# Loading k and v with the token halves of half of the heads exchanged, so that scores skip the masked quarter from tile 6 on, and splitting u and w1 with fewer ScalarE products

## The chip, the cores and the metric

The kernel runs on one core of one Trainium2 chip. The metric is the device time of one execution in microseconds (us), taken from several executions. A *fast* run is one in the undisturbed state; all medians, lowest and highest values below are of fast runs.

## The reference, cut to what matters

Two blocks follow each other. The first is a linear attention with decay (4 batches, 8 heads, 768 tokens, 64 values per head), whose output is laid out as x with 512 columns. The second is a mixing step on x, ending in two large products with w_ch1 (512x2048) and w_ch2 (2048x512).

```python
for b in range(nb):                                   # blocks of tokens
    qb, kb, vb = (q[:, :, sl], k[:, :, sl], v[:, :, sl])
    intra = einsum('bhic,bhjc->bhij', qb, kb) * Dmask     # scores, causal mask with decay
    intra = einsum('bhij,bhjd->bhid', intra, vb)
    inter = einsum('bhid,bhde->bhie', qb * lam_pow, kv_state)
    out[:, :, sl] = intra + inter
    kv_state = lam_block * kv_state + einsum('bhsd,bhse->bhde', kb * rev_pow, vb)
...
u = x + (x.T @ U @ V).T
return u + maximum(u @ w_ch1, 0) @ w_ch2
```

The kernel works in tiles of 128 tokens: 6 per batch, 24 in all. In a tile's 128x128 scores of one head the quarter "late keys, early queries" is wholly masked. That quarter is what the change leaves out.

## The kernel before

Per tile there are three loads (q, k, v), each of all 8 heads: 128 partitions (tokens) by 8 heads by 64 values, 256 KB. Only the loads of the very first tile's q and k are cut in two.

```python
def load(name, s, engine):
    b, c = divmod(s, NT)                                   # NT = 6 tiles per batch
    t = raw_pool.tile([P, H, D], FP32, tag=f"{name}raw", bufs=4 if name == "k" else 3, ...)
    source = {"q": q, "k": k, "v": v}[name]
    n = H if name == "v" else H // parts(s)
    for h in range(0, H, n):
        engine.dma_start(out=t[:, h : h + n, :],
            in_=source[b, h : h + n, c * P : (c + 1) * P, :].rearrange("h p d -> p h d"))
    raw[s, name] = t
...
def load_next(name, engine=nc.sync):                       # all but the very first k on the SyncE queue
    if waiting[name]:
        load(name, waiting[name].pop(0), engine)
```

`load_next` is called where a buffer comes free: q's and k's after the tile's transposes, v's after the state product. The kernel's program order on SyncE is therefore also the order of its DMA queue. The weights' loads ("words") and the stores of finished u tiles stand in the same queue:

```python
def turn(s):
    ...                                                    # 4 transposes on TensorE
    nc.sync.dma_start(out=u_d[s], in_=xs.pop(s))           # frees one of the 9 buffers of x
    ...
def intra(s):
    ...                                                    # 32 passes into px
    xs[s] = x_pool.tile([P, C], FP32, tag="x", name="x_nat")   # bufs=9
    nc.scalar.copy(xs[s].rearrange(...), px)               # ScalarE empties px
```

The scores, and the splitting of u into a high and a low part for the large products:

```python
def scores(s):
    ...
    for a in range(HP):                                    # 4 pairs of heads
        for x in range(2):
            for rows in half if s >= 2 * NT else [slice(0, P)]:
                nc.tensor.matmul(out=pss[rows, x, a, :], lhsT=kt[half[x], a, rows],
                                 rhs=qt[half[x], a, :], start=True, stop=True)
...
    te = tmp("te").rearrange(...)
    nc.scalar.mul(te, t, E)                                # E = 1/4096
    nc.scalar.copy(hi, t)
    nc.gpsimd.tensor_tensor(out=diff, in0=te, in1=low.bitcast(FP32), op=ALU.subtract)
```

## Time and profile before

| | before |
|---|---|
| median of 3 runs | 676.5 us (676.48 to 676.61) |
| span of the profiled run | 674.7 us |
| attention (start to the first instruction of the large products) | 123.3 us |
| DMAs that SyncE issues in attention | 99 |
| time that these issues took | 75.6 us of 123.3 |

The prediction below shows the page, the stretches and the chain. Two views more are needed here. The first is SyncE's own timeline (start, length, line, operation, tile): early in the kernel, where issues stand in a row, and at 82 us, where they come after pauses.

```profile
5.04 0.85 SPq L267 DMA_DIRECT2D kraw<-in_k_dram  x1
5.94 0.85 SPq L267 DMA_DIRECT2D vraw<-in_v_dram  x1
6.83 0.85 SPq L139 DMA_DIRECT2D words<-in_moe_U_dram  x1
...
82.70 0.37 SPq L267 DMA_DIRECT2D qraw<-in_q_dram  x1
83.18 0.52 SPq L267 DMA_DIRECT2D kraw<-in_k_dram  x1
84.93 0.37 SPq L267 DMA_DIRECT2D vraw<-in_v_dram  x1
```

In the early row an issue takes 0.85 us; at 82 us q's and v's take 0.37 after a pause, and k's 0.52, 0.11 us behind q's. The pauses are visible as SyncE's own waits (what its queue waited for: total us, times, longest):

```profile
SPq L267 <- PE pkv L406: 19.7, 14, 3.7
...
SPq L267 <- PE pq L343: 10.4, 10, 2.0
```

In this trace SyncE waits some 30 us for buffers to come free, so it seems to have time to spare. Whether issue times can be read like this is taken up again under whole_loads, where the same 99 DMAs took longer to issue.

### The profile page before, as it was taken

To read this page: it belongs to the slowest core of one execution; us is meant where nothing else is said; L and a number is where in the kernel's file an instruction comes from. 1 tells how busy PE (TensorE), PEld (TensorE's weight loads), DVE (VectorE), ACT (ScalarE), POOL (GpSimd) and SP (SyncE) were. 2 spreads that over 40 slices of the span, in tenths; PEclk is the share of its full clock that TensorE was granted. 3 is DMA by queue.
4 is the path that set the end of the run, shared out by engine and by line. 5 is a ranking of instruction groups with operands and counts; after the bars stand their busy time and mean duration, and the time that the engine had idled before them with its cause. 6 is when DMAs were issued, how large, how long until landed. Compare 5 with 4: busy or idle time off the path is not lost.

```text
span 674.7 us, 13222 instructions
## 1 busy us (share of the span) xinstructions
PE 666.1 (99%) x5124; PEld 545.0 (81%) x5124; DVE 500.1 (74%) x879; ACT 293.3 (43%) x545; POOL 113.8 (17%) x92
## 2 busy tenths in 40 slices
PE   9999999999999999999999999999999999999997
PEld 8888888887888888888888888888888888888885
DVE  5689999777999777777797255786586775865864
ACT  4666878555665544444455121232232322322320
POOL 4556667330000000000000000030030200300300
PEclk9999999999999999999999999999999999999999
DMA  9999894164777655555577999854253363453421
GB/s 203 223 235 248 207 221 124 64 223 155 243 256 244 221 202 204 203 204 203 202 266 258 324 329 373 294 168 154 94 203 109 110 203 94 159 153 95 163 86 63
DMA packets 131776, 131.28 MB, mean 195 GB/s; under 512 B 81346, under 2 KB 89794, under 8 KB 131714
## 3 DMA queue, kind: packets, MB, share of 16 engines
q1 hardware_dynamic: 130656, 130.18, 60.5%
q8 instruction: 40, 0.66, 0.4%
q10 hardware_dynamic: 1058, 0.26, 0.2%
q14 instruction: 22, 0.18, 0.1%
HBM read 80.09 MB, written 50.33 MB: 193 GB/s over the span
## 4 chain that ended last, share of the span: by engine, by line
PE 93%; DVE 3%; ACT 2%; issue 0%; DMA 0%; SPq 0%; DVEq 0%; ACTq 0%
PE pz L709 27%; PE pz L841 13%; PE pz L843 13%; PE pd L719 13%; PE pd L845 13%; PE pss L388 3%; PE px L441 3%; PE put L511 1%; PE pq L343 1%; PE pkv L406 1%; PE px L429 1%; PE pk L343 1%; DVE sm L397 1%; PE pp L456 1%; PE pu L494 1%
## 5 line engine op out<-in xcount | busy, mean ns | idle before, releaser
L709 PE MATMUL pz<-u_hl,w 128*128 128x512 f32 x768 | 190.5, 397 | 0.0
L709 PEld LDWEIGHTS pz<-u_hl,w 128*128 128x128 f32 x768 | 144.0, 188 | 35.5 <-issue 0.4
L841 PE MATMUL pz<-w_hl,m 128*128 128x512 f32 x384 | 151.6, 396 | 0.0
L843 PE MATMUL pz<-w_hl,m 128*128 128x512 f32 x384 | 151.6, 396 | 0.0
L845 PE MATMUL pd<-w_d,m 128*128 128x512 f32 x384 | 150.0, 396 | 0.0
L824 ACT ACTIVATE m<-mt 128x512 fp32r<-128x512 f32 x96 | 60.7, 632 | 195.4 <-PE pd L845 144.6
L825 DVE SCALAR_TENSOR_TENSOR m<-rm,m 128x512 fp32r<-128x512 f32 x96 | 71.5, 746 | 50.1 <-ACT m L824 49.9
L870 POOL TENSOR_TENSOR o<-o,u 128x512 f32<-128x512 f32 x20 | 29.8, 1522 | 447.4 <-DVE o L866 447.4
L724 DVE SCALAR_TENSOR_TENSOR r<-pd,r 128x512 f32<-128x512 f32 x96 | 61.8, 686 | 54.7 <-ACT r L715 43.6
L719 PE MATMUL pd<-u_d,w 128*128 128x512 f32 x384 | 98.6, 397 | 0.0
L843 PEld LDWEIGHTS pz<-w_hl,m 128*128 128x128 f32 x384 | 72.3, 188 | 17.7
L845 PEld LDWEIGHTS pd<-w_d,m 128*128 128x128 f32 x384 | 72.3, 188 | 17.6
L841 PEld LDWEIGHTS pz<-w_hl,m 128*128 128x128 f32 x384 | 72.3, 188 | 17.6
L719 PEld LDWEIGHTS pd<-u_d,w 128*128 128x128 f32 x384 | 72.1, 188 | 17.3
L715 ACT ACTIVATE r<-pz 128x512 f32<-128x512 f32 x96 | 52.0, 594 | 60.0 <-PE pz L709 60.0
L826 DVE SCALAR_TENSOR_TENSOR m<-m 128x512 fp32r<-128x512 f32 x96 | 69.2, 721 | 0.9
L823 DVE TENSOR_SCALAR mt<-rm 128x512 uint32<-128x512 uint32 x96 | 46.2, 481 | 28.2 <-DMA rm<-r_d 27.7
L204 ACT CAST w<-wt 128x512 fp32r<-128x512 f32 x32 | 19.9, 622 | 40.9 <-DVE wt L201 33.7
L397 DVE TENSOR_TENSOR sm<-pss,mask 128x512 f32<-128x512 f32 x48 | 30.8, 684 | 5.3 <-PE pss L388 5.2
L371 POOL TENSOR_TENSOR qs<-qt,powq 128x512 f32<-128x512 f32 x20 | 26.0, 1298 | 23.9 <-ACT qt L346 20.0
L441 PEld LDWEIGHTS px<-vraw,sm 128*64 128x64 f32 x768 | 24.7, 137 | 6.3 <-issue 2.4
L159 ACT ACTIVATE sc<-sc,ends 128x512 f32<-128x512 uint32 x30 | 21.7, 723 | 18.2 <-DVE sc L153 18.2
(84 smaller groups left out, 710.2 us busy)
## 6 DMA issues: line engine op xcount, KB each, us to landing
r_d<-r SPq DMA_DIRECT2D x96, 256.0 KB, 2.3
rm<-r_d SPq DMA_DIRECT2D x96, 256.0 KB, 2.7
words<-in_moe_w_ch_dram SPq DMA_DIRECT2D x30, 512.0 KB, 4.4
w_d<-w SPq DMA_DIRECT2D x16, 768.0 KB, 3.3
w_hl<-w_d SPq DMA_DIRECT2D x16, 512.0 KB, 6.4
vraw<-in_v_dram SPq DMA_DIRECT2D x24, 256.0 KB, 4.1
u_d<-x_nat SPq DMA_DIRECT2D x24, 256.0 KB, 3.2
u<-u_d SPq DMA_DIRECT2D x24, 256.0 KB, 4.0
```

Source lines behind the costliest of these rows:

```text
L441: nc.tensor.matmul(out=px[half[t], x, a, :], lhsT=sm[:, x, a, half[t]], rhs=vr[:, 2 * a + x, :], start=(first and a == 0), stop=(a == HP - 1),
L709: nc.tensor.matmul(out=acc[g][0], lhsT=w[:, n, ct, :], rhs=uhl[g][:, n, ct, :], start=(ct == 0 and n == 0), stop=(ct == CT - 1 and n == 1),)
L715: nc.scalar.mul(rs[g], acc[g][0], 1.0 + E)
L719: nc.tensor.matmul(out=acc[g][1], lhsT=w[:, 2, ct, :], rhs=ud[g][:, ct, :], start=(ct == 0), stop=(ct == CT - 1),)
L724: nc.vector.scalar_tensor_tensor(rs[g], acc[g][1], 4096.0, rs[g], ALU.mult, ALU.add)
L823: nc.vector.tensor_scalar(t.bitcast(U32), r.bitcast(U32), HI, None, ALU.bitwise_and)
L824: nc.scalar.activation(out=m[:, 0], in_=t, func=AF.Relu)
L825: nc.vector.scalar_tensor_tensor(m[:, 1], r, 0.0, hi, ALU.max, ALU.subtract)
L826: nc.vector.scalar_tensor_tensor(m[:, 2], hi, E, low, ALU.mult, ALU.subtract)
L841: nc.tensor.matmul(out=pz, lhsT=m[:, 0, cols], rhs=hl[:, 0], start=first, stop=False)
L843: nc.tensor.matmul(out=pz, lhsT=m[:, 1, cols], rhs=hl[:, 1], start=False, stop=end)
L845: nc.tensor.matmul(out=pd, lhsT=m[:, 2, cols], rhs=dd, start=first, stop=end)
```

## The change

Its intent has two parts.

*Scores.* From tile 6 on the masked quarter is skipped by giving each head two passes: early keys against 128 queries, late keys against 64. To balance the quarters of the array, two of the four pairs of heads keep their tokens with the halves exchanged. This is done in the load: k and v of heads 4 to 7 come in two DMAs of 64 partitions, each landing in the other half. Each k or v load thus becomes three DMAs: 128 partitions of heads 0 to 3, and 64 + 64 partitions of heads 4 to 7. The bytes stay the same. The mask of these heads is built from a turned identity.

*Splitting.* u's high part is kept divided by 4096, which saves ScalarE the product `te`; w1's low part is written by VectorE itself, which saves another ScalarE product.

```diff
@@ load
-        source = {"q": q, "k": k, "v": v}[name]
-        n = H if name == "v" else H // parts(s)
+        source = {"q": q, "k": k, "v": v}[name][:, :, c * P : (c + 1) * P, :]
+        n = H // parts(s) if name == "q" else H // 2
         for h in range(0, H, n):
-            engine.dma_start(
-                out=t[:, h : h + n, :],
-                in_=source[b, h : h + n, c * P : (c + 1) * P, :].rearrange("h p d -> p h d"),
-            )
+            rows = [(slice(0, P), slice(0, P))]
+            if name != "q" and h > 0:
+                rows = [(half[0], half[1]), (half[1], half[0])]
+            for to, of in rows:
+                engine.dma_start(
+                    out=t[to, h : h + n, :],
+                    in_=source[b, h : h + n, of, :].rearrange("h p d -> p h d"),
+                )
@@ scores
-        for a in range(HP):
+        for a in (0, 2, 1, 3):
+            first, last = half[::-1] if a in turned_a else half
+            both = [(first, slice(0, P)), (last, half[1])]
             for x in range(2):
-                for rows in half if s >= 2 * NT else [slice(0, P)]:
+                for rows, cols in both if s >= NT else [(slice(0, P), slice(0, P))]:
                     nc.tensor.matmul(
-                        out=pss[rows, x, a, :], lhsT=kt[half[x], a, rows],
-                        rhs=qt[half[x], a, :], start=True, stop=True,
+                        out=pss[rows, x, a, cols], lhsT=kt[half[x], a, rows],
+                        rhs=qt[half[x], a, cols], start=True, stop=True,
@@ splitting of u
-            te = tmp("te").rearrange("p (c n) -> p c n", n=P)
-            nc.scalar.mul(te, t, E)
-            nc.scalar.copy(hi, t)
-            nc.gpsimd.tensor_tensor(out=diff, in0=te, in1=low.bitcast(FP32), op=ALU.subtract)
+            nc.scalar.mul(hi, t, E)
+            nc.gpsimd.tensor_tensor(
+                out=diff, in0=hi.bitcast(FP32), in1=low.bitcast(FP32), op=ALU.subtract
+            )
@@ the first product's evacuation
-            nc.scalar.mul(rs[g], acc[g][0], 1.0 + E)
+            nc.scalar.mul(rs[g], acc[g][0], 4096.0 + 1.0)
```

Cut: the parameter by which w1 gets the new splitting and w2 keeps its old one, the turned identity and its scans, and keeping one score buffer for all tiles (so that the skipped quarter holds finite numbers).

More of the change, by code (lines that the diff above doesn't have):

```diff
@@ L187, in weight_steps, with split_steps @@
         return fetches + [one, two, three, four]
-    def split_steps(tile_of, src, in_parts=False):
+    def split_steps(tile_of, src, in_parts=False, scale=None):
         st = {}
@@ L206, in six @@
         def six():
-            w = st["w"]
-            nc.vector.tensor_tensor(out=w, in0=w, in1=st["t"], op=ALU.subtract)
-            on_scalar(lambda: nc.scalar.mul(st["o"][:, 1, :], w, 4096.0))
+            w, low = st["w"], st["o"][:, 1, :]
+            st["low"] = low.bitcast(FP32) if scale is None else w
+            nc.vector.tensor_tensor(
+                out=low if scale is None else w, in0=w, in1=st["t"], op=ALU.subtract
+            )
+            if scale is not None:
+                on_scalar(lambda: nc.scalar.mul(low, w, scale))
         def seven():
             nc.vector.scalar_tensor_tensor(
-                st["o"][:, 2, :], st["t"], -E, st["w"], ALU.mult, ALU.add
+                st["o"][:, 2, :], st["t"], -E, st["low"], ALU.mult, ALU.add
             )
@@ L250, in bank @@
         return psa[0].tile(shape, FP32, tag=tag, bufs=2, name=name)
+    half = [slice(0, D), slice(D, P)]
+    turned_a = range(HP // 2, HP)
     lamb = consts.tile([P, H], FP32, name="lamb")
@@ L285 @@
     mask = consts.tile([P, 2, HP, P], FP32, name="mask")
+    ident_turned = consts.tile([P, P], FP32, name="ident_turned")
     rev = small[:, 8:16].rearrange("p (x a) -> p x a", x=2)
@@ L297, in constants @@
                 nc.vector.tensor_tensor_scan(
-                    mask[:, x, a, :], lamb[:, h : h + 1].broadcast_to([P, P]), ident, 0.0,
-                    ALU.mult, ALU.add,
+                    mask[:, x, a, :], lamb[:, h : h + 1].broadcast_to([P, P]),
+                    ident_turned if a in turned_a else ident, 0.0, ALU.mult, ALU.add,
                 )
@@ L323 @@
     st = {}
+    scores_of = []
     kv = {}
-    half = [slice(0, D), slice(D, P)]
     def keep_busy(n):
@@ L383, in scores @@
         qt, kt = st[s]["qt"], st[s]["kt"]
-        st[s]["pss"] = pss = two_banks("pss", "pss").rearrange("p x (a i) -> p x a i", a=HP)
-        for a in range(HP):
+        if s == 0:
+            scores_of.append(two_banks("pss", "pss").rearrange("p x (a i) -> p x a i", a=HP))
+        pss = scores_of[0]
+        for a in (0, 2, 1, 3):
+            first, last = half[::-1] if a in turned_a else half
+            both = [(first, slice(0, P)), (last, half[1])]
             for x in range(2):
-                for rows in half if s >= 2 * NT else [slice(0, P)]:
+                for rows, cols in both if s >= NT else [(slice(0, P), slice(0, P))]:
                     nc.tensor.matmul(
-                        out=pss[rows, x, a, :], lhsT=kt[half[x], a, rows],
-                        rhs=qt[half[x], a, :], start=True, stop=True,
+                        out=pss[rows, x, a, cols], lhsT=kt[half[x], a, rows],
+                        rhs=qt[half[x], a, cols], start=True, stop=True,
                     )
     def masked(s):
-        pss = st[s].pop("pss")
+        pss = scores_of[0]
         st[s]["sm"] = sm = att.tile([P, 2, HP, P], FP32, tag="sm", bufs=1, name="sm")
@@ L529, in rest @@
         def rest():
-            te = tmp("te").rearrange("p (c n) -> p c n", n=P)
-            nc.scalar.mul(te, t, E)
-            nc.scalar.copy(hi, t)
-            nc.gpsimd.tensor_tensor(out=diff, in0=te, in1=low.bitcast(FP32), op=ALU.subtract)
+            nc.scalar.mul(hi, t, E)
+            nc.gpsimd.tensor_tensor(
+                out=diff, in0=hi.bitcast(FP32), in1=low.bitcast(FP32), op=ALU.subtract
+            )
         turned[s] = rest
@@ L654 @@
     make_identity(nc, ident)
+    nc.gpsimd.memset(ident_turned, 0.0)
+    for x in range(2):
+        nc.gpsimd.tensor_copy(out=ident_turned[half[x], half[1 - x]], in_=ident[half[x], half[x]])
     keep_busy(2)
@@ L733, in keep @@
             nc.sync.dma_start(out=w2_d[ft], in_=w2v.pop(ft).bitcast(FP32))
-        return split_steps(tile_of, moe_w_ch2[ft * P : (ft + 1) * P, :]) + [keep]
+        rows = moe_w_ch2[ft * P : (ft + 1) * P, :]
+        return split_steps(tile_of, rows, scale=4096.0) + [keep]
     w2hl, w2dd = {}, {}
```

## The prediction

> **What bounds the kernel now.** I read the page first: which engine is full, and whether the chain that ended last runs through it.
>
> ```profile
> PE 666.1 (99%) x5124; PEld 545.0 (81%) x5124; DVE 500.1 (74%) x879; ACT 293.3 (43%) x545; POOL 113.8 (17%) x92
> ...
> DMA  9999894164777655555577999854253363453421
> ...
> PE 93%; DVE 3%; ACT 2%; issue 0%; DMA 0%; SPq 0%; DVEq 0%; ACTq 0%
> PE pz L709 27%; PE pz L841 13%; PE pz L843 13%; PE pd L719 13%; PE pd L845 13%; PE pss L388 3%; PE px L441 3%; PE put L511 1%; PE pq L343 1%; PE pkv L406 1%; PE px L429 1%; PE pk L343 1%; DVE sm L397 1%; PE pp L456 1%; PE pu L494 1%
> ```
>
> TensorE holds 93% of the chain, and four fifths of it are the two big products (L709, L719, L841 to L845), whose instructions the change leaves alone. It touches the first 123 us, where 24 tiles of attention are worked through; scores (L388) are 3% of the chain, some 20 us. The first slices of the DMA row are full, and become lighter only later in attention.
>
> Second, the busy time by stretches (PE, PEld, DVE, ACT, POOL, then clock, DMA share, GB/s), for who stands just behind TensorE in attention:
>
> ```profile
> 31.00:45.00 14.00, 12.88 (x306) 11.23 (x306) 11.36 (x23) 9.41 (x22) 6.76 (x6) 1.00 0.94 221
> 75.00:96.00 21.00, 21.00 (x542) 19.26 (x537) 19.55 (x32) 17.21 (x39) 16.06 (x13) 1.00 0.85 214
> 150.00:400.00 250.00, 250.00 (x1069) 200.86 (x1068) 190.02 (x339) 123.76 (x216) 2.60 (x2) 1.00 0.66 233
> ```
>
> From 75 to 96 us PE is full, but DVE is at 19.55 of 21 us, 93%, and the clock is full speed. So TensorE can be shortened here by a few per cent at most before DVE takes over. From 150 us on PE is alone.
>
> Third, the chain in order of time (start, length), for what one step (one tile) is made of and where other engines set its end:
>
> ```profile
> 59.19 1.09 PE pss L388 x16
> 60.28 0.62 PE px L429 x32
> ...
> 71.49 0.51 ACT u_hl L532
> 72.00 0.02 issue
> 72.03 0.61 ACT vp L484
> ...
> 74.73 0.69 PE pkv L406 x16
> ...
> 80.15 1.03 PE pss L388 x32
> 81.19 0.46 PE px L429 x32
> ```
>
> Scores take 1.09 us as 16 passes (tiles 0 to 11, one matmul of 64x128 weights per head, two passes each in fp32) and 1.03 us as 32 (tiles 12 to 23, output split in two halves of rows). The old-state product after them (L429, the same 32 passes) takes 0.62 us after the first form and 0.46 after the second. The ACT lines are a place where ACT, not PE, sets the end of a step.
>
> **What the Trainium skill says.** (1) "TensorE: Matmul & The Clock Gate", Part 3 on packing small matmuls: matmuls on different row and column groups of the array run side by side, about 4 ns apart, starts and ends staying in program order. The trace agrees in kind: in tile 21's scores four passes start 6 to 7 ns apart and the next four 109 ns after them; in L429, with 64 columns streamed, fours follow at 58 ns. So time goes with streamed columns: 109 against 58. (2) "TensorEngine Tiling (Array Packing)", Key Properties: changing the tiling mode drains the array. The trace agrees: 0.62 - 0.46 = 0.16 us more for L429 where the mode changes before it. (3) "DMA: Bandwidth & Descriptors", Rules for kernel authors: two transfers to disjoint partition halves are not worth it, use one of 128 partitions. The change does just that split, for k and v; no run shows its cost yet. (4) The same page, Issuing engines are not separate DMA queues: issue time on a sequencer is small against the DMA. In this trace an uncontended issue is 0.37 us for q or v and 0.52 for k, not small once there are three for one.
>
> **The change part by part.**
>
> *Scores.* From tile 6 on each head has one pass pair with 128 streamed columns for its early keys and one with 64 for its late keys; the masked quarter is left out (the score buffer is kept, so what stands there is finite and the mask makes it zero). Turning two pairs of heads balances this: over the order 0, 2, 1, 3 each quarter of the array streams 128, 64, 128, 64 columns. If quarters overlap freely, a tile's eight rounds cost 4 x 109 + 4 x 58 = 668 ns in place of 872: 0.20 us less. Starts in program order hold back some: walking the order by hand with 107 and 53 ns of streaming I get some 690 ns, 0.18 less. I take 0.2. Tiles 6 to 11 also change to the split form, and with it the drain before L429 goes: 1.09 + 0.62 becomes (1.03 - 0.2) + 0.46, 0.42 us less. If all were on the path: 5 x 0.42 + 0.25 + 12 x 0.2 = 4.75 us.
>
> *u's and w1's splitting.* The ACT product te (L531, 635 ns, 16 times) goes, and GpSimd reads hi instead. ACT's product for w1's low part (L209, 632 ns; 16 of 32) goes too, DVE writing the low part itself. Most of it is ACT idle time; it counts only where ACT ends a step, and there it is worth the 0.53 us between te's start and that of the copy after it.
>
> *Added.* One GpSimd memset and two 64x64 copies: the existing memset of this size took 0.21 us, and the mask's scans that read the result start at 3.1 us, 1.8 us after the identity is ready: hidden. Each k and v load becomes three DMAs, 95 more, in the stretch where DMA is at 0.94 to 1.12 of its engines.
>
> *Walking the steps by the chain.* Tiles 6 and 7: nothing, because from 29.5 to 39.98 us the chain is DVE work without a break (masks, V's and the low-rank rows' splitting). Tile 8: PE alone, 0.42. Tile 9: nothing; L441 waits for DVE, which does two w1 operations of 2.4 us ahead of the mask. Tile 10: ACT sets the end through te; 5.2 us falls by 0.53, and PE's part is then as short: 0.55. Tile 11: 0.42. Tile 12: 0.2. Tile 13: ACT again (the lines above; te stands just ahead of them), 0.5. Tiles 14 to 17: DVE's work is 4.74 us per step, continuous from 75.5 to 89.2, beside PE's 4.73 now and 4.53 after; so two or three of four savings come through, 0.5. Tile 18: 0.2. Tile 19: te once more, but DVE's mask is close behind, 0.4. Tiles 20 to 23: 0.6 of 0.8, for the same DVE reason. Sum: 0.42 + 0.55 + 0.42 + 0.2 + 0.5 + 0.5 + 0.2 + 0.4 + 0.6 = 3.8 us.
>
> *Against it, loads.* The early loads have little room:
>
> ```profile
> 25.55 0.59 PE pq L343 x4
> 26.14 0.44 PE pk L343 x4
> 26.57 0.12 issue
> 26.69 1.14 PE px L441 x30
> ```
>
> The 0.12 us of "issue" is a load: v of tile 4 landed at 26.56 us in the trace and L441 started at 26.69. q of tile 3 landed at 16.38 and was used at 16.82. From the start to 53 us the SyncE queue issues without a pause. Its own work per step after the change, from the uncontended issues, is 0.37 for q, about 1.3 for k, 1.1 for v, and 0.4 each for u and a weight load where there are any, with 0.05 between them: about 3.7 to 4.1 us against a step of 4.3 to 4.5. So it keeps up, but each DMA also waits for the one eight issues earlier (the built program shows eight semaphores taken in turn), which is now 0.9 MB in flight in place of 2. I put 0.6 us of lost time on tiles 1 to 5, before the DVE stretch.
>
> Sum: 676.5 - 3.8 + 0.6 = 673.3 us.
>
> **The rivals.**
>
> *DVE becomes the bound.* For it: 93% busy, the masks' ends 0.2 us ahead of L441 in tiles 14, 15 and 21. Against it: there are lighter steps between (tiles 16, 17, 18, 22, 23). Already in my sum; if every step from 14 on is held by DVE, 1.1 us more is lost: 674.4.
>
> *Mixed lengths don't overlap.* If a round of four lasts as long as its longest pass, scores stay at eight rounds of 109 ns. Then tiles 12 to 23 gain nothing from scores and 6 to 11 only the drain and form, 0.22. Left are 0.2 + 0.5 + 0.2 + 0.5 + 0.4 = 1.8 us: 675.3. For it: only equal lengths are seen in this trace. Against it: the fours are only ordered, not locked, in their starts.
>
> *The loads fall behind.* If the queue, at nearly 4 us per step with DMA engines over 90% busy, loses half a us per step over the twelve tiles up to 55 us, PE waits for k and v, and the gain is gone or turns: 677 to 680. For it: the 26.57 us wait and the skill's rule. Against it: the bytes and the 256-byte packets are the same, and the buffers hold three to four tiles, which from 40 us on have landed 6 us before use.
>
> *All of the saving is on the path and loads cost nothing:* 4.75 of scores and 1.5 of ACT can't both count fully, as they overlap in tiles 10, 13 and 19; the most I can make of it is 5.2: 671.3.
>
> **Range and chances.** 673.3 us, 0.5% less than before. 671.5 to 676.0 should hold it 8 times in 10: the low end is nearly everything on the path, the high end the mixed lengths failing with late loads. 2% is 13.5 us, three times what scores and ACT could give, so faster by over 2% has 1%; slower by over 2% needs loads a full 13.5 us behind, 1%; within 2% 98%.
>
> **What would show it.** Scores of tiles 6 to 23 at 0.80 to 0.88 us in the chain, and L429 at 0.46 from tile 7 on: right; 1.03: the second rival. te gone from ACT, steps 10, 13 and 19 shorter by 0.4 to 0.55. The product stretch from 150 us on unchanged to 0.1 us. Waits of L441 or L343 for k or v, above all from 8 to 30 us, would show the loads; later starts of L388 in tile 5 than 28.36 us are their price. More "DVE sm" ahead of L441 from 75 us on would show the first rival. The prediction is wrong in kind if attention ends at or after 123.3 us.

## The result, and the profile after

| | before | with the change |
|---|---|---|
| median | 676.56 us (676.48 to 676.71, 4 runs) | 700.51 us (700.01 to 702.74, 4 runs) |
| ratio of means | 1 | 1.036 (95%: 1.0338 to 1.0383) |
| span of the profiled run | 674.7 us | 698.5 us |
| attention | 123.3 us | 146.6 us |
| SyncE's issues in attention | 99, 75.6 us | 193, 123.3 us |

The outputs are correct. Ratios here and below are the mean time of one kernel's fast runs over that of the other's fast runs of the same rounds, so they are not quite the ratio of the medians quoted. The change costs 3.6%, not the 0.5% gain predicted.

The page of the changed kernel: busy time, the slices for PE and DMA, and the chain by engine.

```profile
PE 669.3 (96%) x5220; PEld 546.1 (78%) x5220; DVE 497.7 (71%) x879; ACT 277.1 (40%) x513; POOL 111.7 (16%) x95
...
PE   8886798899999999999999999999999999999997
...
DMA  6777787716477655555567889965344363353431
...
PE 83%; DMA 7%; SPq 5%; ACT 2%; issue 2%; DVE 1%; POOL 1%; ACTq 0%; DVEq 0%; POOLq 0%
```

ScalarE's part of the change is there (277.1 us after 293.3). PE's share of the chain has fallen from 93% to 83%; DMA and SPq, SyncE's queue, stood at 0% and now hold 12%, most of it loads and stores of attention. The DMA row, though, has become *lighter* in the first slices (6 and 7 where there were nines). The same in three stretches (columns as in the prediction's second fence):

```profile
31.00:45.00 14.00, 11.43 (x267) 9.91 (x268) 9.91 (x18) 6.43 (x12) 6.88 (x6) 1.00 0.69 157
...
60.00:75.00 15.00, 9.89 (x227) 8.52 (x228) 9.80 (x17) 6.35 (x14) 4.92 (x5) 0.89 0.76 187
...
174.00:424.00 250.00, 250.00 (x1069) 201.09 (x1068) 188.83 (x339) 116.25 (x201) 2.09 (x2) 1.00 0.66 231
```

Three readings. The DMA engines moved 157 GB/s where they had moved 221, so they are not what is full. PE is busy for two thirds of the time in the middle of attention. And the product stretch, shifted by the 24 us, is the same to the instruction: 1069 matmuls in 250 us, as before. All of the loss is in attention.

SyncE's timeline in the changed kernel shows a first suspect:

```profile
48.91 0.38 SPq L281 DMA_DIRECT2D qraw<-in_q_dram  x1
49.40 1.83 SPq L281 DMA_DIRECT2D kraw<-in_k_dram  x3
51.33 2.56 SPq L281 DMA_DIRECT2D vraw<-in_v_dram  x3
53.94 0.60 SPq L140 DMA_DIRECT2D words<-in_moe_w_ch_dram  x1
54.63 0.38 SPq L281 DMA_DIRECT2D qraw<-in_q_dram  x1
```

There is no pause left in this stretch. One round, from q to q, takes 5.72 us (54.63 - 48.91), while TensorE's step is 4.62 us where nothing holds it. The chain of waits runs through the queue (start, length, what; "SPq" is an issue):

```profile
51.33 0.55 SPq L281
51.93 1.30 SPq L281
...
53.27 3.10 DMA vraw<-in_v_dram
...
56.52 0.69 PE px L462 x16
...
60.45 0.52 SPq L281
...
61.02 0.60 SPq L281
...
61.67 0.61 SPq L281
...
77.65 4.66 DMA u_d<-x_nat
82.38 0.07 ACT x_nat L467
```

First a v load, issued late, lands at 56.37 us and lets TensorE's px start at 56.52. Later the store of u (u_d<-x_nat) stands behind loads in the queue; it has to land before a buffer of x is free, and ScalarE's copy of px (L467) waits for it. In the view of waits (total us, times, longest) that is a wait which the kernel before does not have; its copy of px waits for TensorE only, whose result it copies:

```profile
ACT x_nat L446 <- PE px L441: 18.9, 20, 2.3
```

After:

```profile
ACT x_nat L467 <- DMA u_d<-x_nat: 26.8, 10, 7.0
ACT x_nat L467 <- PE px L462: 19.0, 13, 3.6
...
PE px L462 <- DMA vraw<-in_v_dram: 4.7, 8, 1.3
```

A second loss rides on the first: in two stretches around the end of a pause of TensorE (2.6 us up to 63.3, 3.3 us up to 84.0) the granted clock was lower, 0.66 from 62 to 67 us and 0.72 from 82 to 88 us. That costs at most 0.34 x 5 + 0.28 x 6 = 3.4 us of TensorE's time. A pause of 3.2 us at 109 us had no such dip, so no rule is drawn from the two. Once the loads are done a step takes 4.62 us again (tile 22 to 23).

### The profile page after: what moved, and what is told of

It reads as the page before. It is cut to its first block, busy times and chain, and to the rows that moved or that the text cites. A ratio compares the mean times of both kernels' runs of the same rounds, so it can differ in the third digit from the quotient of the medians.

```text
span 698.5 us, 13527 instructions
## 1 busy us (share of the span) xinstructions
PE 669.3 (96%) x5220; PEld 546.1 (78%) x5220; DVE 497.7 (71%) x879; ACT 277.1 (40%) x513; POOL 111.7 (16%) x95
## 4 chain that ended last, share of the span: by engine, by line
PE 83%; DMA 7%; SPq 5%; ACT 2%; issue 2%; DVE 1%; POOL 1%; ACTq 0%; DVEq 0%; POOLq 0%
PE pz L733 26%; PE pd L743 13%; PE pz L868 12%; PE pz L866 12%; PE pd L870 12%; SPq L281 4%; PE px L462 2%; DMA rm<-r_d 2%; DMA vraw<-in_v_dram 2%; DMA u_d<-x_nat 1%; PE put L532 1%; DMA kraw<-in_k_dram 1%; PE pss L409 1%; PE pp L477 1%; PE px L450 1%
## 5 line engine op out<-in xcount | busy, mean ns | idle before, releaser
L462 PE MATMUL px<-vraw,sm 128*64 128x64 f32 x768 | 30.3, 230 | 7.8 <-DMA vraw<-in_v_dram 4.7
L462 PEld LDWEIGHTS px<-vraw,sm 128*64 128x64 f32 x768 | 26.2, 141 | 14.4 <-DVE sm L418 4.7
L467 ACT COPY x_nat<-px 128x512 f32<-128x512 f32 x24 | 14.0, 585 | 45.8 <-DMA u_d<-x_nat 26.8
```

The costliest lines, as they stand in the source:

```text
L462: nc.tensor.matmul(out=px[half[t], x, a, :], lhsT=sm[:, x, a, half[t]], rhs=vr[:, 2 * a + x, :], start=(first and a == 0), stop=(a == HP - 1),
```

## The experiments

Two theories stood at first. *Theory 1*: cutting the loads is the whole loss, and either (1a) it is the issue time on SyncE's one queue, or (1b) all queues share what SyncE's lacks, so that moving DMAs to another one does not help. *The rivals*: the turned heads or mixed pass lengths (scores, the kept score buffer, masks) lose the time (A, B), or the pieces are slow as transfers (C, D, and theory 2 of the last run). The texts on record use these names. The runs of one group shared a chip.

I read from each trace, besides the page, when tile 2's scores and tile 23's start: the first shows what the start lost, the difference the steady part.

### Which part costs: four runs

**whole_loads**: the change, but k and v loaded whole and not turned. The result is wrong on purpose (relative error 0.82), since the turned heads get unturned data; the instructions elsewhere are those of the change.

```diff
-        n = H // parts(s) if name == "q" else H // 2
+        n = H if name == "v" else H // parts(s)
         for h in range(0, H, n):
-            rows = [...]; for to, of in rows: engine.dma_start(...)
+            engine.dma_start(out=t[:, h : h + n, :], in_=source[b, h : h + n, c * P : (c + 1) * P, :]...)
```

> The changed kernel with k and v loaded whole, in one DMA each, so the rows of half of the heads are not turned: wrong results on purpose, all else as changed. Theory 1: the loss is gone, and what is left is my prediction's gain of 3.8 us without its 0.6 us for loads: 672 to 674 us; scores of tiles 6 to 23 at 0.72 to 0.76 us from their first start to that of the next group, old-state products after them without the 0.16 us drain. Rival A: 695 us or more. Rival B, mixed lengths run in lockstep: 675 to 676 us.

Measured: 673.34 us (672.22 to 676.65), ratio 0.9948 (0.993 to 0.9966). Everything but the loads gives the predicted gain, nearly to the digit. Its chain:

```profile
86.80 0.82 PE pss L405 x22
88.18 0.59 PE put L528 x4
89.87 1.08 PE px L458 x32
```

The scores are 0.82 us where they were 1.03 or 1.09. Mixed lengths do overlap. So the loads cost 700.5 - 673.3 = 27 us.

The same trace warns against reading SyncE's timeline too directly. With the 99 DMAs of the kernel before, its issues take 94.9 us of the 119.2 us of attention (96.4 in splitting_only's trace, against 75.6 before), up to 100 us it has only two pauses over 0.12 us, and nothing is lost:

```profile
L277 SPq DMA_DIRECT2D vraw<-in_v_dram x24: 367/1970/2777, 3.0 to 106.8; - x24
```

Here the numbers of a line are durations in ns: least, median, most. A v load that can be issued in 0.37 us typically took 1.97 us. So an issue can stretch without costing time, and a queue without pauses, or the sum of its issues, does not prove that the queue is the bound. What stretches an issue no run shows. The proof has to come from runs that take DMAs off the queue.

**splitting_only**: the kernel before with the new splitting of u and w1 alone (that part of the diff above; w2's stays).

> The kernel before with only the second part of the change: u's high part kept divided by 4096, w1's low part written by DVE, te gone. Theory: ACT sets the end of a step only in tiles 10, 13 and 19, where 0.53 us each go: 674.5 to 675.5 us. Rival: ACT's chain is replaced at once by PE or DVE, which stand just behind: 676.0 to 676.6 us.

Measured: 675.54 us (674.66 to 677.2), ratio 0.998 (0.9973 to 0.9987), correct. It gains 1.35 us (0.2% of 676.8) and lies 0.04 us above the range expected, below the rival's 676.0.

**cut_loads**: the kernel before with k and v in the change's three DMAs, but each half landing in its own place.

```diff
+                rows = [(half[0], half[0]), (half[1], half[1])]
```

> The kernel before, with nothing but each k and v load cut into three DMAs as in the change, rows not turned; right results. Theory 1, the SyncE queue: in the changed kernel a DMA issued behind another takes 0.60 us of the queue and 0.05 to the next whatever its size, so a step needs about 5.5 us of it against 4.7 us of TensorE; the whole loss comes from the loads. Expected 698 to 704 us, with u's stores late and ACT waiting for them as in the changed kernel. Rival A, the score passes of mixed length, the turned order or the kept score buffer cost the time on TensorE: 676 to 679 us here.

Measured: 702.42 us (701.55 to 704.49), ratio 1.0376 (1.036 to 1.0393), correct. Cutting the loads alone loses 25.6 us, without a turned head anywhere. Cutting is the loss, and neither turning nor scores have a share that shows.

**cut_v**: the same for v only.

```diff
+            if name == "v" and h > 0:
+                rows = [(half[0], half[0]), (half[1], half[1])]
```

> The kernel before with only v's loads cut in three (48 DMAs more, half of the change's). Theory 1, a queue with a threshold: a step needs 0.5 us for q, 0.9 for k, 1.9 for v, 0.4 for u's store and 0.65 for a weight load where there is one, 3.7 to 4.4 us, which is still below TensorE's 4.3 to 4.9: 676 to 683 us, far less than half of the loss. Rival C, the DMA engines move the small pieces more slowly, in proportion to their number: half of the loss, 687 to 690 us.

Measured: 684.37 us (682.95 to 688.26), ratio 1.0098 (1.0082 to 1.0114), correct. It lies just above the 676 to 683 expected: 7.5 us for half of the pieces, against 25.6 us for all, under a third. A queue with slack would behave so: the first additions go partly into its slack, the later ones all onto the path. In proportion to the pieces, as rival C had it, the loss would have been 12.8 us.

### The number of DMAs, or their form: three runs

**cut_by_heads**: three DMAs for k and v, of heads 0-3, 4-5 and 6-7, each of all 128 partitions.

```diff
+        cuts = [0, 4, 6, 8] if name != "q" else list(range(0, H + 1, n))
+        for h, end in zip(cuts, cuts[1:]):
             engine.dma_start(
+                out=t[:, h:end, :], in_=source[b, h:end].rearrange("h p d -> p h d")
```

> The kernel before with each k and v load cut into three DMAs of all 128 partitions, by heads (4, 2 and 2), as many DMAs of the same sizes as in cut_loads. Theory 1, only the number of DMAs counts: 700 to 705 us as in cut_loads. Rival D, transfers of half of the partitions are the costly thing: 680 us or less.

Measured: 690.71 us (689.01 to 691.41), ratio 1.02 (1.0181 to 1.0218), correct. It lies outside what was expected: the same 193 DMAs lose 14 us, not 25.6. The number alone does not decide. SyncE's view of this kernel's v loads, then of the changed kernel's:

```profile
L269 SPq DMA_DIRECT2D vraw<-in_v_dram x72: 367/470/1626, 4.8 to 126.0; - x72
```

```profile
L281 SPq DMA_DIRECT2D vraw<-in_v_dram x72: 374/602/1867, 5.6 to 136.6; - x72
```

The median is 470 ns for this kernel's pieces, all of 128 partitions, and 602 for the change's. Taking the three pieces of a v load apart in the changed kernel's trace (medians of the last 20 tiles): 0.55 us for the one of 128 partitions, 0.60 and 0.62 for the two of 64; in cut_by_heads 0.42, 0.51 and 0.47.

**two_by_rows**: the kernel before with k and v in two DMAs of 64 partitions by 8 heads. **two_by_heads**: in two DMAs of 128 partitions by 4 heads.

```diff
 two_by_rows
+            for rows in half:
+                engine.dma_start(out=t[rows], in_=source[b, :, rows, :].rearrange("h p d -> p h d"))
 two_by_heads
-        n = H if name == "v" else H // parts(s)
+        n = H // parts(s) if name == "q" else H // 2
```

> The kernel before with each k and v load in two DMAs of 64 partitions and all 8 heads. It is to tell why the cut by heads lost 14 us and the cut with rows 26: in their traces a piece of 64 partitions took 0.60 us of the queue, one of 128 partitions 0.47 to 0.52. Theory 1 as mended, the queue's time per DMA counts and is longer for 64 partitions: about 0.48 + 4 x 0.65 + 0.45 (u) + 0.65 (weights) = 4.2 us per step, near the step's length: 677 to 684 us. Rival D, half-partition transfers move slowly as such (all bytes of k and v here): 690 us or more.

> The kernel before with each k and v load in two DMAs of 128 partitions, 4 heads each: as many DMAs as two_by_rows, 48 fewer than cut_by_heads. Theory 1 as mended: about 0.48 + 4 x 0.53 + 0.45 + 0.5 = 3.6 us per step, under every step of TensorE: 676 to 679 us, and less than two_by_rows. If only the number of DMAs counted, the two runs would be the same.

Measured: two_by_rows 683.36 us (681.79 to 684.86), ratio 1.0091 (1.0072 to 1.011); two_by_heads 678.78 us (677.87 to 680.66), ratio 1.0027 (1.0015 to 1.0038); both correct, before beside them 677.2. Both as expected. The same number of DMAs and of bytes: halving by partitions costs 6.2 us, halving by heads 1.6. SyncE's view, by rows:

```profile
L269 SPq DMA_DIRECT2D vraw<-in_v_dram x48: 595/627/2552, 3.7 to 118.2; - x48
```

By heads:

```profile
L268 SPq DMA_DIRECT2D vraw<-in_v_dram x48: 368/512/2266, 3.5 to 113.7; - x48
```

No 64-partition issue of SyncE took under 0.595 us, even with twice the heads; a 128-partition one takes 0.368 at its best. So the floor goes with the partitions and not with the bytes or rows moved. The typical values lie closer for k: 0.670 us by rows, 0.640 by heads, with least values of 0.596 and 0.492. Why the floor differs is not shown by any run. Rival D's 690 us or more, for all of k and v moved in halves, did not come.

### Another queue: four runs

If SyncE's issuing is what is short, DMAs moved to ScalarE's queue must win time, with the same pieces. Four kernels are the change with

```diff
 q_on_act        load_next: nc.scalar if name == "q" and len(waiting["q"]) < NS - 3 else engine
 q_u_on_act      the same, and the u stores of attention: nc.scalar.dma_start(out=u_d[s], ...)
 k_on_act        load_next: nc.scalar if name == "k" else engine
 k_late_on_act   load_next: nc.scalar if name == "k" and len(waiting["k"]) < NS - 4 else engine
```

The last one moves k from tile 4 on only; it was made because k_on_act lost 9.3 us up to tile 2.

> The changed kernel with the q loads after the first three issued from ScalarE's queue, all pieces as in the change; right results. Theory 1a, SyncE's own issuing is the bound: it sheds some 0.5 us of about 5.5 to 6 per step, so the loss of 27 us against the whole loads falls by 24 steps x 0.4 to 0.5: 686 to 692 us. Theory 1b, both queues share one maker of descriptors, so the number of DMAs counts whoever issues them: 698 us or more.

> As q_on_act, and u's stores during attention issued from ScalarE too, which no longer stand behind the loads. Theory 1a: SyncE is down to about 3.8 us per step, 4.4 with a weight load, under TensorE's 4.6; ScalarE takes on some 0.9 us of about 4: 675 to 681 us. Theory 1b: 696 us or more.

> The changed kernel with all k loads issued from ScalarE's queue, three per step. Theory 1a: SyncE is down to 3.7 us per step and free, but ScalarE, in order, takes on 1.8 us on top of 3.6 to 4.2, so it becomes the bound at some 5.5 us per step: 684 to 696 us, with ACT the engine that others wait for in attention. Theory 1b: 698 us or more, and the pieces issued by both take longer than 0.65 us each.

> The changed kernel with k's three loads per tile moved to the ScalarE queue from tile 4 on only, so that the start is the change's own (in the run with all of k there, ScalarE stood 11.5 us for a k load at the start). Theory 1, the one queue is short of issue time: the start costs about 3.0 us as in the change (tile 1's scores at 13.5 us in place of 10.5), and from tile 1 to tile 23 the loss should be near the 5.8 us that the trace with all of k on ScalarE shows (111.25 us in place of 105.45 with whole loads), not the change's 24.4. Sum 673.3 + 3.0 + 5.8 = 682, range 679 to 685; SyncE's issues then take about 75 of 128 us. Theory 2, the pieces themselves are late (each piece or its transfer costs the same on any queue, or ScalarE is blocked as much as SyncE was): no better than the 688 to 690 of the runs with q or all of k moved.

All four are correct. The losses in the last two columns are against whole_loads (tile 2's scores at 14.79 us, tile 23's 101.15 us later), worked out from one trace each:

| kernel | median (lowest to highest) | ratio (95%) | SyncE's issues in attention | lost up to tile 2 | lost from tile 2 to 23 |
|---|---|---|---|---|---|
| change | 700.51 (700.01 to 702.74) | 1.036 (1.0338 to 1.0383) | 193, 123.3 of 146.6 us | 3.5 | 23.8 |
| q_on_act | 688.78 (687.98 to 690.12) | 1.0178 (1.0162 to 1.0194) | 172, 110.3 of 136.2 us | 4.0 | 13.0 |
| q_u_on_act | 689.15 (687.29 to 692.53) | 1.0187 (1.0156 to 1.0219) | 156, 106.5 of 132.8 us | 5.8 | 7.8 |
| k_on_act | 690.36 (687.63 to 691.55) | 1.0194 (1.017 to 1.0218) | 124, 74.0 of 134.3 us | 9.3 | 5.8 |
| k_late_on_act | 686.47 (684.59 to 687.57) | 1.0138 (1.0114 to 1.0162) | 133, 83.9 of 133.4 us | 7.2 | 7.0 |

By their times, q_on_act fell where theory 1a expected it, and k_on_act in its wide range; q_u_on_act missed clearly (675 to 681 was expected), and k_late_on_act missed by 1.5 us (679 to 685), though it is better than the rival's 688 to 690. None came near the 696 to 698 us or more of theory 1b.

The steady column shows why. The more was taken from SyncE, the less was lost from tile 2 on: 23.8 us, then 13.0, and 5.8 to 7.8 in the other three. This is SyncE's queue; the pieces and the bytes are the same. One figure needs a correction: q_on_act's trace has a granted clock of 0.50 from 59.5 to 69.7 us, which is at most 5.1 us of its 13.0, as the dips above are at most 3.4 of the change's 23.8. So the order among the four moved kernels is not shown, their distance from the change is. Nor do the runs tell SyncE's own issue time from whatever stands behind its queue and can make an issue wait: a DMA on ScalarE gets around both. The u store's price comes off too. Waits of ScalarE's copy of px for the store, in q_on_act:

```profile
ACT x_nat L467 <- DMA u_d<-x_nat: 16.4, 5, 6.9
```

In k_late_on_act:

```profile
ACT x_nat L467 <- DMA kraw<-in_k_dram: 8.5, 3, 3.9
...
ACT x_nat L467 <- DMA u_d<-x_nat: 2.0, 2, 1.7
```

The 26.8 us of the change have become 16.4 and then 2.0. The second view also shows the price of the cure: ScalarE's queue issues in program order, between its copies, so a copy now stands behind k's DMAs (8.5 us). At the start, where all buffers are still filling, that price is highest; in k_on_act (the line gives ScalarE's idle time before its first instruction):

```profile
ACT L362 <- DMA kraw<-in_k_dram: 11.5, 1, 11.5
```

ScalarE issued twelve k pieces in a row, from 1.3 to 11.4 us, before its first copy, and the first scores started at 13.5 us in place of 6.2. This is what the expectations of q_u_on_act and k_late_on_act left out: each assumed that what leaves SyncE's queue costs nothing on ScalarE's. In q_u_on_act SyncE is also still without a pause from about 59 to 82 us, with some issues of over 1 us and 7 pieces per tile left on it. Why single issues take 1 to 2.5 us (they occur in the kernel before too) I could not settle.

### A version better than both

**split_from_6**: splitting_only, and the two-half form of the scores from tile 6 on instead of 12, with nothing turned and the loads whole.

```diff
-                for rows in half if s >= 2 * NT else [slice(0, P)]:
+                for rows in half if s >= NT else [slice(0, P)]:
```

> A version meant to beat both: the kernel before with the second part of the change (as splitting_only) and scores in the two-half form from tile 6 instead of 12, nothing turned, loads whole. The old-state product after them loses its drain: 0.2 us in those of tiles 7 to 11 where TensorE sets the step (8, 10, 11): 674.5 to 675.5 us, up to 1 us under splitting_only's 675.5. If DVE or ACT take it over at once: 675.5.

Measured: 675.48 us (674.28 to 676.89, 19 runs), ratio 0.9975 (0.9968 to 0.9982), before beside it 677.2; correct. It beats the kernel before by 0.25% and the change by 3.6%. The 0.998 of splitting_only lies so close that the earlier split of the scores is not shown to add anything. Turning in two DMAs instead of three (64 partitions by both groups of heads) was not tried.

## Why the prediction was wrong

**The step that failed** is "Against it, loads", in the prediction's words: "So it keeps up". Its term is "I put 0.6 us of lost time on tiles 1 to 5"; measured it is 27 us (700.5 against 673.3 for the same kernel with whole loads). Its other term there, that each DMA waits for the one eight issues earlier, did not act: in the changed kernel's trace none of SyncE's issues in attention started before that one had landed (of those whose landing is in the trace), and at most 6 were under way.

- *The input of that step was wrong.* It took 0.37 us for q or v and 0.52 for k as an issue's own cost, all of them of 128 partitions. q's 0.38 held in the changed kernel's rows; v's 0.37 had been seen after a pause. The step's sum from the changed kernel's trace: q 0.38, k 0.64 + 0.60 + 0.61, v 0.55 + 0.60 + 0.62, u 0.54, weights 0.60, and nine gaps of 0.05, together 5.6 us, against the 3.7 to 4.1 of the prediction and TensorE's 4.6. It is an estimate made of trace medians; the trace's own round of 5.72 us has one long issue in it.
- *That sum is not the whole loss.* Not every tile has a weight load and a u store. In the changed kernel's trace attention ends 27.3 us later than in whole_loads (146.6 against 119.2). Of its issues 16 took over 1 us, together 13.3 us more than at 0.60 each. So, as an estimate, up to 13 of the 27 us may go to stretched issues, whose cause is open, and the rest to the typical ones.
- *It was readable beforehand that 0.37 was not v's cost in a row.* The early row of 0.85 us issues was in the trace, and up to 54 us no v issue took under 0.73. The prediction even says that SyncE issues without a pause up to 53 us, with 3 loads per tile in place of 7, and still took only "uncontended" times. Full DMA engines may explain the early row: from 4 to 8 us the DMA share was 1.19, and 269 GB/s were moved. But after a change that makes the queue busier, the cost in a row is the one to take, and the pieces' own form had no measurement at all. With nothing to take a 64-partition issue from, the range should have been wider.
- *The rival "The loads fall behind" named the right mechanism and the wrong size*: "half a us per step over the twelve tiles up to 55 us" and 677 to 680. It fell behind by about 1.1 us per step on average (23.8 us over 21 steps), and in jumps: three steps (tiles 9 to 10, 12 to 13, 17 to 18) hold 11.2 us of it, while from tile 13 to 16 nothing was lost. It was held down by "the buffers hold three to four tiles". Buffers only delay a shortage of rate; they don't cure it. And it saw only loads late for TensorE, not the u stores in the same queue, whose wait (26.8 us on ScalarE) became the longest one.
- *The skill pointed at it and was discounted.* The prediction cited the rule on disjoint partition halves, and wrote that no run showed its cost. There is one more place it should have opened: the Trainium skill, "Perfetto Trace Analysis", section What "DMA-bound" means, names as one of three bounds the sequencer of the issuing engine, its track solid with DMA slices. SyncE's track in the changed kernel is nearly that: 123.3 of 146.6 us, and 13 us more are gaps of at most 0.12 us between issues. But in whole_loads it is as solid up to 100 us and nothing is lost, so here the sign pointed to the queue without proving it.

**The steps that held**, all read from whole_loads:

- *The sum of the gains*: 3.8 us predicted, 3.5 measured (0.52% of 676.8). Its parts came out differently, as the next point shows, so a match this close is partly luck.
- *Its parts shifted.* Scores plus the old-state product went from 1.50 us (0.924 + 0.575, first start to the next group's first start) to 1.39 (0.76 + 0.626) in tiles 14 to 17: 0.11 us per tile, not 0.2. The product after the scores did not come down to 0.46, or 0.575 in this measure; mixed scores leave 0.05 us more to wait for there (in the chain it takes 0.56 us, where split_from_6, with scores of one length, has the 0.46). In tiles 8, 9 and 11 the pair went from 1.72 to 1.39 us, 0.33 instead of 0.42. In exchange the step of tile 13 to 14 fell by 0.52 us (5.889 to 5.367) and that of 19 to 20 by 0.53, where 0.5 and 0.4 were predicted. Some 0.3 us of the gain comes before tile 1's scores (10.49 us in place of 10.81), where the prediction saw nothing to gain; whether that is the change or a difference between two executions is open.
- *"Mixed lengths don't overlap"* was rightly given little: 0.76 us in place of 0.92 for the scores.
- *"DVE becomes the bound"* did not come: from 75 to 96 us DVE was busy 20.31 of 21 us in whole_loads, and tiles still ran at 4.62 to 4.66 us.
- *The product stretch is unchanged*, as predicted. The prediction's last sentence, "wrong in kind if attention ends at or after 123.3 us", is what happened.

What stays open: why 64 partitions cost more to issue than 128, what stretches single issues beyond 1 us (in whole_loads without a loss), whether SyncE's issuing itself or something behind its queue is short, and how much of the remaining 5.8 to 7.8 us of the moved-queue kernels is SyncE and how much ScalarE.

## What to carry to other kernels

Before cutting a load into pieces, add up the issuing queue's work for one step of the loop, every DMA in it, stores and weights too, with typical durations that issues show *in a row* and in the form that the change will use; if the sum comes near the step, the queue may be the next bound, however light the DMA engines are. A timeline without pauses does not decide it, since issues stretched without a loss in whole_loads; move some DMAs to another queue and see whether time comes back. In an in-order queue the damage appears at whatever stands behind the loads, here a store that frees a buffer. Prefer a cut that keeps all 128 partitions, and measure a new form of DMA alone before trusting a gain elsewhere.

## What the Trainium skill lacked or had wrong

- "DMA: Bandwidth & Descriptors", Rules for kernel authors: the rule against two transfers to disjoint partition halves holds here, but its reason (they share the same DMA engines) does not show in the traces as what cost the time. In two_by_rows the DMA engines' share was 0.82 from 31 to 45 us and 0.87 from 75 to 96, where the kernel before had 0.94 and 0.85; the issue of a 64-partition piece took at least 0.595 us, of a 128-partition one 0.368. Halving by partitions cost 6.2 us, halving by heads 1.6.
- The same page, Issuing engines are not separate DMA queues: that issuing on several engines saves only the issue time, usually small against the DMA, misleads for a kernel with 193 DMAs in 147 us. There the issues fill 123 us, stretched ones included; moving 21 of them to ScalarE saved 11.7 us (700.5 to 688.8).
- "Perfetto Trace Analysis", DMA Optimizations: its advice to balance DMAs over the engines that can issue them where the issuing engine is full agrees with that. What it lacks is the price: in one run ScalarE issued k pieces for 10.1 us before its first copy, and in another its copies stood 8.5 us behind k's DMAs.
- No page that I read tells what an issue takes on this chip by its form, in a row: typically 0.42 to 0.55 us for a cut v piece of 128 partitions and 0.60 to 0.62 for one of 64, with some 0.05 between; or that an issue can stretch without a loss, as v's whole loads did (0.37 us at least, 1.97 typically).
- "TensorE: Matmul & The Clock Gate", Part 3, tells nothing of packed passes of unequal length. Passes of 128 and 64 columns, mixed, took 0.76 us for a tile's scores in place of 0.92: 18% less, where a quarter of the columns was left out.
